# Storing the turned gated tile from the tile that held z1, and queueing the last such store behind the last stage's first loads

## The chip, the cores and the metric

The kernel runs on one core of one Trainium2 chip. Its engines work side by side, each through its own list of instructions in order: PE (TensorE, matrix products, into PSUM), ACT (ScalarE), DVE (VectorE), POOL (GpSimd) and SP (SyncE, which here only issues DMAs; POOL and ACT issue some too). They wait for each other by semaphores. The metric is the device time of one execution in microseconds (us); the number to beat is the median of three runs.

## What is computed

x is 2048 x 512, float32. It is layer-normed, and two mixers are added to it:

```python
x = A_x
xn = _layernorm(x, axis=-1)
return x + _A_ref(xn, wqkv, w_phi, wo) + _B_ref(xn, w_in, w_sp, b_sp, w_out)

# A: linear attention, 32 heads of 16
q, k, v = qkv[0], qkv[1], qkv[2]
phi_q = concat(softmax(q @ w_phi), softmax(-(q @ w_phi)))      # phi_k alike
o = phi_q (phi_k^T v) / (phi_q (phi_k^T 1) + 1e-6);   A = o @ wo

# B: gated MLP, Fh = 688
z = gelu(xn @ w_in);  z1 = z[..., :Fh];  z2 = layernorm(z[..., Fh:])
g = w_sp @ z2 + b_sp                                            # w_sp is 2048 x 2048
B = (z1 * g) @ w_out
```

## The kernel before

Rows are tiled by 128 (16 tiles, `NT`). Every float32 operand of a large product is split into two float32r parts, high and low, and a product is three matmuls (`mm3`, L53 to L55): high by high, high by low, low by high. The high part is a rounding copy (`round_h`, L45, mostly on ACT), the low part a subtraction (`rest_l`, L49, on DVE). Nearly all such work has the lines L45 and L49, so it is told apart by its tiles.

There are three stages. The first makes v, the features of k and q, and the raw z1, which goes to DRAM (`z1_d`). The middle stage makes z2 and then g = w_sp z2 by Strassen-like products of two by two blocks. The last stage, for each pair of row tiles, makes (z1 * g) @ w_out and o @ wo and adds both to x.

The part around the change is the product g and what follows it.

- g has eight steps (i = 0 to 7), each a pair of row tiles; each step has four chunks (32 chunks, `NC`). A chunk needs a pair of w_sp tiles from DRAM (`wf`, two loads of 256 KB on SP, L512, issued three chunks ahead) and their sums `S` and parts `A` (`prep_a`, on DVE and ACT, two chunks ahead). `products` gives seven PSUM tiles `g` (P1, P2, P6, P5, P7, P3, P4, made in that order), in 8 banks that are used in turn.
- At a step's end `drain` (L710 to L715) reads the seven tiles into the tile `c`: one ACT copy, then seven adds on DVE. L715 reads P7.
- `gate` (L721 to L735) multiplies that with the gelu of z1, splits off the last 48 columns, turns the whole in blocks of 32 (`dve.transpose`, L732) and stores it to DRAM (`u_d`) with four DMAs on SP, whose elements are 128 bytes. z1 comes by two loads on POOL's queue (`load_z1`, L692) into the tile tagged `z1`. Both tiles, `c` and `z1`, have one buffer. In the kernel before, the product goes into `z1`, the turned tile goes back into `c`, and the store reads `c`.
- Step 7 goes otherwise: its drained tile is kept, and its gate comes late in the last stage (`GATE_LAST`).
- During the last chunks, buffers of the operand `B` that PE has read for the last time are taken again (`slot`) for what the last stage needs first: w_out's parts, the turned tile 0 (`first_gate`: tiles `u_uh` and `ul_rt`), the normalizer `zb`, finished features of q (`first_q`: `eq`), and raw ones (`load_q`: `et`), which `q_fin` (seven DVE operations, L487 to L494, the first writing `qtmp`) finishes.
- The last stage: `project_u` (17 matmuls into `pout`), `attend_T` (16 transposes into `ptq`, L860, or L858 where the source is `et`), `attend` (products `po`, L875, copied out as `oT`), `project_o` (12 matmuls more into `pout`, with `wo`'s parts `woh` and `wol`), then the add of x and the store.

What sets the order: the program is written as loops, and a scheduler with a model of its own places the instructions of each engine; `tc.issue_after(x)` keeps what follows it behind x. DMA completions are counted in eight lanes for those that SP and ACT issue, used in turn, so that a DMA also waits for the landing of the one eight before it.

Of the kernel before, what the change touches and what calls it, by code (L numbers as in the profile page):

```python
# [10 lines left out]
F32 = mybir.dt.float32  # L11
F32R = mybir.dt.float32r
AF = mybir.ActivationFunctionType
ALU = mybir.AluOpType
# [23 lines left out]
def mixer(ctx: ExitStack, tc: tile.TileContext, x, x_t, wv, wqkT, phi_bd, wo, w_in, wst, b_r, w_out, out):  # L38
# [9 lines left out]
    def rest_l(l, src, h, eng=None):  # L48
        return (eng or dve).tensor_tensor(l, src, h.bitcast(F32), op=ALU.subtract).ins  # L49
# [427 lines left out]
    QW = NF + 7 * H  # L477

    def load_q(s, et):
        sp.dma_start(et[:, :NF + 2 * H], e_d[s])  # L480
        return et

    def q_fin(et, tmp, zb):
# [222 lines left out]
    def drain(i, g, cb):  # L706
        g = {k: t[:, :FC] for k, t in g.items()}
        b1, b2 = (bias[:, 2 * i + k:2 * i + k + 1] for k in range(2))
        c11, c12, c21, c22 = (cb[:, k] for k in range(4))
        add = lambda o, p, b, q: dve.scalar_tensor_tensor(o, p, b, q, op0=ALU.add, op1=ALU.add)  # L710
        first = act.activation(c12, g["P1"], AF.Copy)
# [3 lines left out]
        dve.tensor_tensor(c21, g["P7"], c21, op=ALU.add)  # L715
        add(c22, g["P5"], b2, c21)
        add(c12, g["P3"], b1, c12)
        drained = add(c21, g["P4"], b2, c21)
        return cb, first.ins, drained.ins

    def gate(i, cb, z, zt):  # L721
        cb, first, _ = cb
        with tc.issue_after(first):
            act.activation(z[:, :, :FH], z[:, :, :FH], AF.Gelu_apprx_tanh)
# [4 lines left out]
        dve.tensor_copy(rh, z[:, :, rm])  # L729
        rest_l(z[:, :, FH:FH + REM], z[:, :, rm], rh)  # L730
        dve.tensor_copy(z[:, :, rm], rh.bitcast(F32))
        dve.transpose(zt, z.rearrange("p k f -> p (k f)"))  # L732
        dst = u_d[2 * i:2 * i + 2].rearrange("k (j a) t -> a (k j) t", a=BL)
        for b in range(0, P, BL):
            sp.dma_start(dst[:, :, b:b + BL], zt[b:b + BL].rearrange("p (m b) -> p m b", b=BL))  # L735
# [50 lines left out]
    for n in range(NC):  # L786
        i = SEQ[n][0]
        if n % NQ == 1 and i < NP - 1:
            z = load_z1(i)
        products(n, g)  # L790
        if n % NQ == NQ - 1 and i < NP - 1:
            c = gt.tile([P, 2 * FU], F32, tag="c", name="c")
            gate(i, drain(i, g, c[:, :4 * FC].rearrange("p (a b) -> p a b", a=4)), z, c)
            g = {}
        if n + 3 < NC:
            raw[n + 3] = load_a(n + 3)
        if n + 2 < NC:
            A[n + 2] = prep_a(n + 2, raw.pop(n + 2))
        if n == NC - 4:
            stage_w()  # L800
        if n == NC - 3:
            zs = slot("zb", F32R)
            zb, ident_r = zs[:, :NF].bitcast(F32), zs[:, NF:NF + P]
            round_h(act, ident_r, ident)
            sp.dma_start(zb, zb_d)
# [14 lines left out]
    us, fin = {}, []  # L820

    def fetch_u(i):
        return load_u(i, cw.tile([P, KF, P], F32, tag="u", bufs=4, name="u"),
# [21 lines left out]
    sp.dma_start(kvT.rearrange("p g t -> p (g t)"), kvT_d)  # L845
    pst = ctx.enter_context(psum("pst", 4))
    pso = ctx.enter_context(psum("pso", 1))

    def attend_T(s):

# [69 lines left out]
    fin.append(ins)  # L920
    features(3)
    for s in (2, 3):
        us[s] = fetch_u(s)

    def ahead(i):

        if 3 < i + 3 < NT:
# [6 lines left out]
    for i in range(0, NT, 2):  # L934
# [17 lines left out]
                z = load_z1(NP - 1)  # L952
        if i == GATE_LAST:
            with tc.issue_after(lasts[0]), tc.issue_after(lasts[1]):
                gate(NP - 1, cb, z, gt.tile([P, 2 * FU], F32, tag="zt", name="zt"))
            p2.close()
        if i + 2 < NT:
            with tc.issue_after(lasts[4]):
# [34 lines left out]
```

## Time and profile before

| | |
|---|---|
| median of 3 runs | 641.39 us (641.39 to 642.18) |
| the profiled execution | 643.36 us, its span 641.6 us, granted clock 0.995 |
| PE busy | 626.9 us (98% of the span) |
| DVE busy | 517.2 us (81%) |
| ACT busy | 269.8 us (42%) |
| the product g | 283 to 499 us of the span |
| the last stage | about 499 us to the end |

PE is nearly always busy, so what can be won is where it waits or runs at a lower clock; an average over the span doesn't show those places, a list of PE's waits does. A row of the timeline is: start in us, length in us, engine, line, operation, out<-in, shapes, count; in brackets the engine's idle time before it and what ended that.

### The profile page before, as it was taken

What the parts mean: (1) busy time and instruction counts of PE and PEld (TensorE: products, weight loads), DVE (VectorE), ACT (ScalarE), POOL (GpSimd) and SP (SyncE); (2) the same over time, 40 slices, a digit from 0 to 9 for tenths busy, and PEclk for the clock granted to TensorE, in tenths of its full rate; (3) what the DMA queues carried; (4) which work ended last, traced back from release to release, by engine and by line L of the source; (5) the groups of instructions that cost most, each with busy time, mean ns of one, the idle gap of its engine ahead of it and who ended that gap; (6) DMA issues with size and microseconds to landing.
All of it is one profiled execution on the core that took longest, in us unless ns stands there. A gap on an engine that the chain in (4) does not pass through costs nothing.

```text
span 641.6 us, 11420 instructions
## 1 busy us (share of the span) xinstructions
PE 626.9 (98%) x4406; PEld 567.6 (88%) x4406; DVE 517.2 (81%) x916; ACT 269.8 (42%) x431; POOL 86.0 (13%) x168
## 2 busy tenths in 40 slices
PE   8999999999999999999999999999999699999997
PEld 6888888888889999999999999999999577777776
DVE  5999979987978779889979687696967589899822
ACT  5644434443423648876443333334334132323220
POOL 4142212111010025350000000000000001100000
PEclk9999999999999999999999999999999799999999
DMA  8445464354256930003474563827567797986930
GB/s 314 159 100 140 123 173 137 99 154 126 67 137 172 331 115 34 2 11 86 139 165 96 143 142 101 178 82 161 125 160 180 243 277 251 336 265 216 260 102 33
DMA packets 94965, 98.39 MB, mean 153 GB/s; under 512 B 52448, under 2 KB 65504, under 8 KB 94912
## 3 DMA queue, kind: packets, MB, share of 16 engines
q1 hardware_dynamic: 84992, 62.81, 35.0%
q0 software_dynamic: 7616, 29.23, 16.1%
q10 hardware_dynamic: 2304, 5.64, 2.3%
q8 instruction: 34, 0.56, 0.4%
q14 instruction: 19, 0.16, 0.1%
HBM read 56.37 MB, written 26.61 MB: 129 GB/s over the span
## 4 chain that ended last, share of the span: by engine, by line
PE 94%; DMA 2%; DVE 2%; issue 1%; SPq 0%; ACT 0%; POOL 0%; DVEq 0%; ACTq 0%; POOLq 0%
PE g L53 10%; PE g L54 10%; PE g L55 10%; PE proj L55 7%; PE proj L53 7%; PE proj L54 7%; PE zps L55 6%; PE zps L53 6%; PE zps L54 6%; PE pout L53 6%; PE pout L54 5%; PE pout L55 5%; PE po L875 2%; DMA wf<-in_wst 1%; PE ptq L860 1%; PE kvps L312 1%
## 5 line engine op out<-in xcount | busy, mean ns | idle before, releaser
L53 PE MATMUL g<-B,A 128*128 128x344 f32 x448 | 143.8, 321 | 2.3 <-DVE c L715 2.3
L54 PE MATMUL g<-B,A 128*128 128x344 f32 x448 | 143.4, 320 | 0.0
L55 PE MATMUL g<-B,A 128*128 128x344 f32 x448 | 143.0, 320 | 0.0
L53 PEld LDWEIGHTS g<-B,A 128*128 128x128 f32 x448 | 84.2, 188 | 3.7 <-DVE c L715 3.5
L54 PEld LDWEIGHTS g<-B,A 128*128 128x128 f32 x448 | 84.2, 188 | 0.0
L55 PEld LDWEIGHTS g<-B,A 128*128 128x128 f32 x448 | 84.2, 188 | 0.0
L45 ACT ACTIVATE A<-S 128x512 fp32r<-128x512 f32 x64 | 40.2, 631 | 82.0 <-DVE S L531 59.6
L113 ACT ACTIVATE e<-e,r_x 128x1024 f32<-128x1024 f32 x28 | 32.2, 1149 | 49.2 <-DVE e L112 49.2
L53 PE MATMUL proj<-wqk_h,xT 128*128 128x512 f32 x128 | 51.0, 398 | 0.0
L55 PE MATMUL proj<-wqk_h,xT 128*128 128x512 f32 x128 | 50.6, 396 | 0.0
L54 PE MATMUL proj<-wqk_l,xT 128*128 128x512 f32 x128 | 50.3, 393 | 0.0
L49 DVE TENSOR_TENSOR A<-S,A 128x512 fp32r<-128x512 f32 x64 | 43.8, 686 | 5.7 <-ACT A L45 5.5
L53 PE MATMUL zps<-w_0h,xT 128*128 128x344 f32 x128 | 41.5, 324 | 0.0
L55 PE MATMUL zps<-w_0h,xT 128*128 128x344 f32 x128 | 41.2, 322 | 0.0
L53 PE MATMUL zps<-w_1h,xT 128*128 128x344 f32 x128 | 41.1, 321 | 0.0
L55 PE MATMUL zps<-w_1h,xT 128*128 128x344 f32 x128 | 40.9, 320 | 0.0
L54 PE MATMUL zps<-w_0l,xT 128*128 128x344 f32 x128 | 40.9, 320 | 0.0
L54 PE MATMUL zps<-w_1l,xT 128*128 128x344 f32 x128 | 40.9, 319 | 0.0
L45 ACT ACTIVATE A<-wf 128x512 fp32r<-128x512 f32 x64 | 31.7, 515 | 20.1 <-PE g L55 10.0
L116 DVE TENSOR_REDUCE sm<-e 128x64 f32<-128x1024 f32 x28 | 33.9, 1209 | 4.9 <-ACT e L113 4.8
L530 DVE TENSOR_TENSOR S<-wf 128x256 f32<-128x256 f32 x32 | 13.4, 420 | 29.6 <-DMA wf<-in_wst 29.6
L49 DVE TENSOR_TENSOR A<-wf,A 128x512 fp32r<-128x512 f32 x64 | 35.3, 552 | 2.3 <-ACT A L45 2.0
(202 smaller groups left out, 1414.2 us busy)
## 6 DMA issues: line engine op xcount, KB each, us to landing
wf<-in_wst SPq DMA_DIRECT2D x64, 256.0 KB, 3.8
e_d<-e POOLq DMA_DIRECT2D x16, 544.0 KB, 5.1
et<-e_d SPq DMA_DIRECT2D x16, 544.0 KB, 5.8
zacc<-e POOLq DMA_DIRECT2D x12, 512.0 KB, 4.7
er<-et POOLq DMA_DIRECT2D x12, 512.0 KB, 4.7
z_d<-z1f ACTq DMA_DIRECT2D x16, 344.0 KB, 3.2
z1t<-z_d POOLq DMA_DIRECT2D x16, 344.0 KB, 5.2
u_d<-c SPq DMA_DIRECT2D x28, 184.0 KB, 6.9
```

What stands on the lines that cost most here:

```text
L45: return act.activation(h, src, AF.Copy).ins
L49: return (eng or dve).tensor_tensor(l, src, h.bitcast(F32), op=ALU.subtract).ins
L53: pe.matmul(dst, ah, bh, start=start, stop=False)
L54: pe.matmul(dst, ah, bl, start=False, stop=False)
L55: return pe.matmul(dst, al, bh, start=False, stop=stop).ins
L113: act.activation(e, e, AF.Exp, scale=scale)
L116: dve.tensor_reduce(sm, heads(e), axis=AX.X, op=ALU.add)
L312: i = pe.matmul(kv_acc[k:k + QP, m // 4], vs[:, m * QP:(m + 1) * QP], e[:, m * HP:(m + 1) * HP], start=first and m < 4 and len(ready) == n ...
L530: dve.tensor_tensor(sums[:, 0], b[:, 0], b[:, 1], op=ALU.add)
L860: pe.transpose(pt[:, a, k].bitcast(F32R), src, ident_r)
L875: lasts[3] = pe.matmul(po[r][c * QP:(c + 1) * QP, k], kvT[rows, m // 2, cols], fs[m // 4][rows, m // 2 % 2], start=True, stop=True).ins
```

## The change

1. `gate` takes two tiles more by name: the product goes into the tile of the drained sums (`u`, that is `c`), and the turned tile into `ut`, which is z1's own tile `z`. The store therefore reads `z1`'s buffer instead of `c`'s. For step 7 the product stays in `z`, as before.
2. `gate` returns its store as a function. Steps 0 to 5 call it at once. Step 6's store is called after the first loads of the last stage: tiles 0 and 1 of `u_d`, two finished and two raw tiles of q.
3. These loads are put together differently: tile 1 of `u_d` goes to a slot of its own (`u1`) ahead of the last chunk, instead of a buffer of the last stage; `q_fin` of tile 2 stands behind the drain of step 7.
4. `wo` comes by four loads of 128 rows instead of sixteen of 32 rows; the loads of tiles 2 and 3 of `u_d` stand ahead of it.
5. The PSUM pool of `pout` and `po` is opened ahead of that of `ptq`, so that it takes the first banks that the product g leaves.

The core of the diff:

```diff
 def load_q(s, et):
-    sp.dma_start(et[:, :NF + 2 * H], e_d[s])
+    load_q.last = sp.dma_start(et[:, :NF + 2 * H], e_d[s]).ins
...
-    def gate(i, cb, z, zt):
+    def gate(i, cb, z, u, ut):
...
-        dve.tensor_tensor(zs, zs, cb.rearrange("p (k j) f -> p k j f", k=2), op=ALU.mult)
+        us = u[:, :, :FH].rearrange("p k (j f) -> p k j f", j=2)
+        dve.tensor_tensor(us, zs, cb, op=ALU.mult)
...
-        dve.transpose(zt, z.rearrange("p k f -> p (k f)"))
-        dst = u_d[2 * i:2 * i + 2].rearrange("k (j a) t -> a (k j) t", a=BL)
-        for b in range(0, P, BL):
-            sp.dma_start(dst[:, :, b:b + BL], zt[b:b + BL].rearrange("p (m b) -> p m b", b=BL))
+        dve.transpose(ut.rearrange("p k f -> p (k f)"), u.rearrange("p k f -> p (k f)"))
+        def store():
+            src = ut.rearrange("p k f -> p (k f)")
+            dst = u_d[2 * i:2 * i + 2].rearrange("k (j a) t -> a (k j) t", a=BL)
+            for b in range(0, P, BL):
+                sp.dma_start(dst[:, :, b:b + BL], src[b:b + BL].rearrange("p (m b) -> p m b", b=BL))
+        return store
...
-            c = gt.tile([P, 2 * FU], F32, tag="c", name="c")
-            gate(i, drain(i, g, c[:, :4 * FC].rearrange("p (a b) -> p a b", a=4)), z, c)
+            c = gt.tile([P, 2, FU], F32, tag="c", name="c")
+            cq = c[:, :, :FH].rearrange("p k (j f) -> p k j f", j=2)
+            store = gate(i, drain(i, g, cq), z, c, z)
+            if i < NP - 2:
+                store()
...
             uT = [first_gate(0)]
-            ets[2] = load_q(2, slot("et"))
-            es[2], last = q_fin(ets.pop(2), slot("qtmp")[:, :NF], zb)
+            es[0], es[1] = first_q(0), first_q(1)
         if n == NC - 2:
-            es[0], es[1] = first_q(0), first_q(1)
-            ets[3] = load_q(3, slot("et"))
-    cb = drain(NP - 1, g, slot("c").rearrange("p (a b) -> p a b", a=4))
+            t = slot("u1", F32R)
+            us = {1: load_u(1, k_tiles(t[:, :KF * P]).bitcast(F32), t[:2 * REM, KF * P:(KF + 1) * P])}
+            ets[2], ets[3] = (load_q(s, slot("et")) for s in (2, 3))
+            with tc.issue_after(load_q.last):
+                store()
+    cb = drain(NP - 1, g, slot("c").rearrange("p (k j f) -> p k j f", k=2, j=2))
+    with tc.issue_after(cb[1]), tc.issue_after(cb[2]):
+        es[2], last = q_fin(ets.pop(2), slot("qtmp")[:, :NF], zb)
...
-    us[1] = fetch_u(1)
...
-    pst = ctx.enter_context(psum("pst", 4))
     pso = ctx.enter_context(psum("pso", 1))
+    pst = ctx.enter_context(psum("pst", 4))
...
+    for s in (2, 3):
+        us[s] = fetch_u(s)
...
         for c in range(ND):
-            rows = [(m * QP, (m + 1) * QP) for m in range(c // 2 * 8 + c % 2, (c // 2 + 1) * 8, 2)]
-            load_w(wo, rows, wo_h[:, c], wo_l[:, c], cw.tile([P, D], F32, tag="wof", bufs=4, name="wof"))
+            t = cw.tile([P, D], F32, tag="wof", bufs=4, name="wof")
+            sp.dma_start(t, wo.rearrange("(k m a r) d -> k a m r d", k=2, a=2, r=QP)[c // 2, c % 2])
+            round_h(act, wo_h[:, c], t)
+            rest_l(wo_l[:, c], t, wo_h[:, c])
```

What this does to the order, first on SP's queue from the last chunks of g into the last stage. In the kernel before (`zb` is the normalizer, `u_d<-c` the store of step 6; behind the last row come the sixteen loads of wo):

```order
L805 DMA zb<-zb_d 128x1024
L735 DMA u_d<-c 32x46x32 x4
L750 DMA u_uh<-u_d 128x5x128
L751 DMA ul_rt<-u_d 96x128
L480 DMA et<-e_d 128x1088
L772 DMA eq<-e_d 128x1024 x2
L480 DMA et<-e_d 128x1088
L750 DMA u<-u_d 128x5x128
L751 DMA rt<-u_d 96x128
L845 DMA kvT<-kvT_d 128x512
```

And in the changed kernel, from the same load of `zb` on (`u_5477` is the slot `u1`; behind the last row come four loads of `u` and `rt` for tiles 2 and 3, and then the four loads of wo):

```order
L812 DMA zb<-zb_d 128x1024
L754 DMA u_uh<-u_d 128x5x128
L755 DMA ul_rt<-u_d 96x128
L776 DMA eq<-e_d 128x1024 x2
L754 DMA u_5477<-u_d 128x5x128
L755 DMA u_5477<-u_d 96x128
L480 DMA et<-e_d 128x1088 x2
L739 DMA u_d<-z1t 32x46x32 x4
L855 DMA kvT<-kvT_d 128x512
```

The four DMAs of the store moved from ahead of seven loads to behind them, and wo has four issues where there were sixteen.

Second, DVE at the drain of step 7 (`c<-g`). Before, the operations of `q_fin` of tile 2 (`qtmp`, `et`) stand ahead of it and between its adds:

```order
L49 TENSOR_TENSOR ul_rt<-u_uh 128x640
L487 TENSOR_TENSOR qtmp<-et,zb 128x1024
L488 TENSOR_REDUCE et<-qtmp 128x64
L710 SCALAR_TENSOR_TENSOR c<-g,bias,c 128x344
L713 TENSOR_TENSOR c<-g,c 128x344
L489 TENSOR_TENSOR et<-et 128x64
L714 TENSOR_TENSOR c<-g,c 128x344
L490 SCALAR_TENSOR_TENSOR et<-et 128x32
L715 TENSOR_TENSOR c<-g,c 128x344
```

In the changed kernel, from the same `ul_rt` on, the last split of an operand `A`, the whole drain, and only then `q_fin`:

```order
L49 TENSOR_TENSOR ul_rt<-u_uh 128x640
L49 TENSOR_TENSOR A<-S,A 128x512
L710 SCALAR_TENSOR_TENSOR c<-g,bias,c 128x344
L713 TENSOR_TENSOR c<-g,c 128x344
L714 TENSOR_TENSOR c<-g,c 128x344
L715 TENSOR_TENSOR c<-g,c 128x344
L710 SCALAR_TENSOR_TENSOR c<-g,bias,c 128x344 x3
L487 TENSOR_TENSOR qtmp<-et,zb 128x1024
L49 TENSOR_TENSOR ul<-u_5477,uh 128x640
L488 TENSOR_REDUCE et<-qtmp 128x64
```

The drain went ahead of `q_fin`; on ACT likewise the rounding of `u_uh` went one place forward, ahead of the last rounding of an `A`.

Third, DVE at the first pair of the last stage, from the first `oT` on. Before, the two adds of x (`xr<-pout`) stand inside `q_fin` of tile 3:

```order
L49 TENSOR_TENSOR oT<-po,oT 128x2x256 x2
L487 TENSOR_TENSOR qtmp<-et,zb 128x1024
L488 TENSOR_REDUCE et<-qtmp 128x64
L489 TENSOR_TENSOR et<-et 128x64
L906 TENSOR_TENSOR xr<-pout,xr 128x512
L490 SCALAR_TENSOR_TENSOR et<-et 128x32
L491 RECIPROCAL et<-et 128x32
L492 TENSOR_TENSOR et<-et 128x64
L906 TENSOR_TENSOR xr<-pout,xr 128x512
L494 TENSOR_TENSOR et<-et 128x1024
```

In the changed kernel they stand behind it and behind the first operation of tile 4's:

```order
L49 TENSOR_TENSOR oT<-po,oT 128x2x256 x2
L487 TENSOR_TENSOR qtmp<-et,zb 128x1024
L488 TENSOR_REDUCE et<-qtmp 128x64
L489 TENSOR_TENSOR et<-et 128x64
L490 SCALAR_TENSOR_TENSOR et<-et 128x32
L491 RECIPROCAL et<-et 128x32
L492 TENSOR_TENSOR et<-et 128x64
L494 TENSOR_TENSOR et<-et 128x1024
L487 TENSOR_TENSOR qtmp<-et,zb 128x1024
L916 TENSOR_TENSOR xr<-pout,xr 128x512 x2
```

So the adds that empty the first two `pout` moved five operations back. PE's list at this place has the sixteen transposes of the next pair in one piece ahead of `project_u`, where before four stood ahead of it and twelve behind it. In steps 0 to 5 of g the order on every engine is as before; what differs there are the tiles.

More of the change, by code (lines that the diff above doesn't have):

```diff
@@ L708, in drain @@
         b1, b2 = (bias[:, 2 * i + k:2 * i + k + 1] for k in range(2))
-        c11, c12, c21, c22 = (cb[:, k] for k in range(4))
+        c11, c12, c21, c22 = (cb[:, k, j] for k in range(2) for j in range(2))
         add = lambda o, p, b, q: dve.scalar_tensor_tensor(o, p, b, q, op0=ALU.add, op1=ALU.add)
@@ L725, in gate @@
         zs = z[:, :, :FH].rearrange("p k (j f) -> p k j f", j=2)
[L726 removed]
+        us = u[:, :, :FH].rearrange("p k (j f) -> p k j f", j=2)
+        dve.tensor_tensor(us, zs, cb, op=ALU.mult)
         rm = slice(KF * P, FH)
         rh = gt.tile([P, 2, REM], F32R, tag="rh", name="rh")
[L729 to L735 removed]
+        dve.tensor_copy(rh, u[:, :, rm])
+        rest_l(u[:, :, FH:FH + REM], u[:, :, rm], rh)
+        dve.tensor_copy(u[:, :, rm], rh.bitcast(F32))
+        dve.transpose(ut.rearrange("p k f -> p (k f)"), u.rearrange("p k f -> p (k f)"))
[5 more added lines that the diff above has]
+        return store
     def slot(name, dt=F32):
@@ L819, in mixer @@
     wk = ctx.enter_context(left("cwk", 2))
-    us, fin = {}, []
+    fin = []
     def fetch_u(i):
@@ L845, in mixer @@
     sp.dma_start(kvT.rearrange("p g t -> p (g t)"), kvT_d)
+    pso = ctx.enter_context(psum("pso", 1))
     pst = ctx.enter_context(psum("pst", 4))
-    pso = ctx.enter_context(psum("pso", 1))
     def attend_T(s):
@@ L921, in mixer @@
     features(3)
-    for s in (2, 3):
-        us[s] = fetch_u(s)
     def ahead(i):
@@ L954, in mixer @@
             with tc.issue_after(lasts[0]), tc.issue_after(lasts[1]):
-                gate(NP - 1, cb, z, gt.tile([P, 2 * FU], F32, tag="zt", name="zt"))
+                gate(NP - 1, cb, z, z, gt.tile([P, 2, FU], F32, tag="zt", name="zt"))()
             p2.close()
```

## The prediction

> **What bounds the kernel now.** I read the page first, then the waits of PE, then the timelines of PE, DVE, SP and ACT where g gives way to the last stage, and last one boundary between two steps of g. The page: the span, and the granted clock in 40 slices.
>
> ```profile
> span 641.6 us, 11420 instructions
> PEclk9999999999999999999999999999999799999999
> ```
>
> One slice of 16 us (497 to 513) has a lower clock. PE's waits, longest first, name the same place at their head, and another one behind it:
>
> ```profile
> PE pout L53 <- DVE c L715: 5.8, 1, 5.8
> PE g L53 <- DVE c L715: 2.3, 4, 0.7
> ```
>
> The first is the start of the last stage, the second are four boundaries between steps of g. The timeline of PE at the first (start, length):
>
> ```profile
> 498.62 0.32 PE L55 MATMUL g<-B,A 128*128 128x344 f32 x1
> 504.78 0.77 PE L53 MATMUL pout<-wu,u_uh 128*128 128x512 f32 x1 [5.84 <-DVE c L715]
> ...
> 511.32 1.48 PE L860 MATMUL ptq<-zb,eq 128*128 128x128 f32 x16
> 512.63 0.46 PE L53 MATMUL pout<-wu,uh 128*128 128x512 f32 x1
> ...
> 516.74 1.09 PE L875 MATMUL po<-f,kvT 64*32 64x256 f32 x32
> 518.57 0.50 PE L53 MATMUL pout<-woh,oT 128*128 128x512 f32 x1 [0.74 <-ACT oT L45]
> ```
>
> PE stands for 5.84 us. Then the first `project_u` takes 511.32 - 504.78 = 6.54 us, and the second, the same 17 matmuls, 516.74 - 512.63 = 4.11 us. Stretches with the granted clock (after the counts) tell why:
>
> ```profile
> 476.00:498.00 22.00, 22.00 (x140) 22.00 (x141) 17.27 (x33) 8.20 (x16) 0.00 (x0) 1.00 0.76 188
> 504.00:508.00 4.00, 3.22 (x8) 2.58 (x9) 4.00 (x10) 0.74 (x1) 0.00 (x0) 0.50 0.57 155
> 512.00:516.00 4.00, 4.00 (x25) 3.39 (x24) 1.58 (x3) 4.00 (x9) 0.00 (x0) 1.00 0.85 247
> ```
>
> Full clock to the end of g, half after the stand, full again later: 6.54 - 4.11 = 2.43 us more lost. Why PE stands, from DVE:
>
> ```profile
> 497.15 0.83 DVE L49 TENSOR_TENSOR ul_rt<-u_uh 128x640 fp32r<-128x640 f32 x1 [4.61 <-ACT u_uh L45]
> 500.01 1.23 DVE L487 TENSOR_TENSOR qtmp<-et,zb 128x1024 f32<-128x1024 f32 x1 [2.03 <-DMA eq<-e_d]
> ...
> 502.40 0.57 DVE L710 SCALAR_TENSOR_TENSOR c<-g,bias,c 128x344 f32<-128x344 f32 x1
> ...
> 504.12 0.52 DVE L715 TENSOR_TENSOR c<-g,c 128x344 f32<-128x344 f32 x1
> ```
>
> DVE sits in its order before `qtmp`, whose tile `et` lands at 500.0; the drain stands behind that, and PE's first `pout` waits for the bank that L715 empties. The late landing comes from SP's queue:
>
> ```profile
> 483.81 0.34 SPq L805 DMA_DIRECT2D zb<-zb_d  x1
> 487.47 4.57 SPq L735 DMA_DIRECT2D u_d<-c  x4
> 492.13 0.65 SPq L750 DMA_DIRECT2D u_uh<-u_d  x1
> ...
> 498.96 11.56 SPq L745 DMA_DIRECT2D wof<-in_wo  x16
> ```
>
> From 484.15 to 487.47 the queue waits for step 6's turned tile, then issues its store for 4.57 us; all first loads come behind. Note the sixteen issues of wo: 11.56 us.
>
> **The change, part by part.** *Drain ahead of `q_fin`, last store behind the first loads.* `u_uh`, `ul_rt` and the two `eq` follow `zb` as soon as PE frees their slots, within the chunk that ends near 485.6 (a chunk is 42 matmuls of 22 / 140 = 0.157 us, 6.6 us, and the last ends at 498.9). So `u_uh` is issued about 7.5 us earlier. The drain's add of P7 then waits for nothing but P7, which PE ends about 2 us before the last product; the adds behind it are done some 0.7 us after the last product. PE needs none of these for its first `pout`: it starts when g ends. Gain 5.84 us, and with no stand the clock stays, as it does over the 0.74 at 518.57 and the 0.7 of the boundaries: 2.43 us. Together 8.27 us. ACT now rounds `u_uh` ahead of the last `A`; the A has room, since its product comes 3.8 us into the last chunk (496.1) and `u_uh` should land by 490.
>
> *What is late next.* `project_u(0)` would run from 498.9 to 503.0, the transposes to 504.3, `project_u(1)` to 508.4, `po` to 509.5, `project_o` from 510.3 (518.57 - 8.27). It needs wo's parts:
>
> ```profile
> 513.73 2.21 ACT L45 ACTIVATE woh<-wof 128x512 fp32r<-128x512 f32 x4
> ```
>
> Tile 1's `u`, before the last of the loads behind the store, is now issued near 487 and lands long before DVE wants it. The store then goes out at about 491.2, when PE has freed the slots of both `et`, and lands 7.0 us later (below); kvT, tiles 2 and 3 and the four loads of wo follow, wo issued about 499.8 to 501.4 and landed by about 506, as four 256 KB loads behind a store take 4.4 to 4.7 us (the wf row below). ACT reaches `woh` behind four copies at about 505.5 and is done at 507.7: some 2.5 us to spare. The four loads instead of sixteen save no time by themselves here (before, woh waited for ACT, not for wo), but the earlier `woh` needs them: sixteen issues of 0.72 us would end past 510. Taken: 0; bounds 0 and 1.5 us lost, if the queue runs 4 us later.
>
> *PSUM banks.* With the drain done 0.7 us after g, the order of the pools decides at most that 0.7 us. Inside the 8.27.
>
> *The turned tile in z1's buffer*, six boundaries. Before (one boundary; SP, POOL, ACT, DVE, PE):
>
> ```profile
> 458.98 6.49 SPq L735 DMA_DIRECT2D u_d<-c  x4
> 459.48 1.07 POOL L692 DMA_DIRECT2D z1t<-z_d  x2 [26.29 <-DVE S L531]
> 468.49 0.46 ACT L711 ACTIVATE c<-g 128x344 f32<-128x344 f32 x1 [2.84 <-DMA u_d<-c]
> 468.84 1.34 ACT L724 ACTIVATE z1t<-z1t 128x1376 f32<-128x1376 f32 x1
> 470.08 0.62 ACT L45 ACTIVATE A<-wf 128x512 fp32r<-128x512 f32 x1
> 471.51 0.42 DVE L530 TENSOR_TENSOR S<-wf 128x256 f32<-128x256 f32 x1 [5.40 <-DMA wf<-in_wst]
> 473.77 0.68 DVE L49 TENSOR_TENSOR A<-wf,A 128x512 fp32r<-128x512 f32 x1
> 475.39 0.51 DVE L715 TENSOR_TENSOR c<-g,c 128x344 f32<-128x344 f32 x1
> 475.96 0.42 PE L53 MATMUL g<-B,A 128*128 128x344 f32 x1 [0.42 <-DVE c L715]
> ```
>
> The chain that ends in PE's wait is store, wf loads behind it, DVE's sums, drain. The change frees `c` early, which ends ACT's 2.84 us of waiting, worth nothing since DVE is later. But it makes POOL's load of z1 wait for the store, and all that ACT holds behind the gelu waits too. Landings, of the last store (no z1 load beside it), of the one above, and of that z1 load and the four wf behind it:
>
> ```profile
> L735 SPq DMA_DIRECT2D u_d<-c x4: 322/884/2329, 487.5 to 489.7; - x4
> DMA to landing us min/median/max: 2.8/4.2/4.7
> ...
> L735 SPq DMA_DIRECT2D u_d<-c x4: 325/932/4168, 459.0 to 461.3; - x4
> DMA to landing us min/median/max: 2.9/6.9/7.3
> ...
> DMA to landing us min/median/max: 4.8/5.0/5.2
> ...
> DMA to landing us min/median/max: 4.4/4.5/4.7
> ```
>
> Alone, a store is down 489.7 + 4.7 - 487.5 = 7.0 us after its first issue; with z1 beside it 9.4 (468.4, since ACT's copy at 468.49 waited for it, less 459.0). So now: store down at 459.0 + 7.0 = 466.0; z1's second load issued 0.6 later (half of 1.07, and 0.1), landed 5.0 later, 471.6; gelu, `A<-wf` 1.24 later (470.08 - 468.84) and 0.62 long, DVE's L49 at 473.5 against 473.77. The wf loads come some 2 us earlier, so L530 no longer decides. Net about 0.2 earlier per boundary, 0.1 us for each of the four that PE feels: 0.5 in all. Bounds: 2.3 us gained (all four waits), 3 us lost (z1 half a us later at six boundaries).
>
> *The last stage's first pairs.* The matmuls `po` at the first two pairs of whole length, and at a later one:
>
> ```profile
> 529.93 1.88 PE L875 MATMUL po<-f,kvT 64*32 64x256 f32 x32
> 546.60 2.10 PE L875 MATMUL po<-f,kvT 64*32 64x256 f32 x32
> 579.49 1.09 PE L875 MATMUL po<-f,kvT 64*32 64x256 f32 x32
> ```
>
> Twice 0.8 to 1.0 us are lost because twelve transposes stand right ahead of `po`, which waits for their copies. With all sixteen ahead of `project_u` that should go: 1.8 us. Against it, DVE's two adds of x now come behind `q_fin` of tile 3 and its next operation; PE needs their `pout` back for the third `project_u`. By DVE's lengths (1.2 us for each of the three long operations, about 1.1 for the four short ones) they end near 518.2, `project_o` near 516, transposes take 1.3: a wait of 0.5 to 1 us, and the copy `er` for tile 5 may come as late again. Taken: 0.5 gained; bounds 1.8 gained, 1 lost.
>
> Sum: 8.27 + 0.5 + 0.5 = 9.3 us. The profiled execution took 643.36 (span 641.6), 1.97 above the median; the sum is a difference within its span, and I take it off the median: 641.39 - 9.3 = 632.1. A change under 0.2% (1.3 us) can't be told from none.
>
> **Rivals.**
> *A, slower: z1 lands late at every boundary.* Behind the store it meets four wf loads of 256 KB, and ACT, then DVE, then PE wait. z1 beside the store cost the store 9.4 - 7.0 = 2.4 us, so that much engine time it needs; if the wf loads halve its rate throughout, it lands 2.4 us later, PE goes on at 478.1 instead of 475.96, six times 2.2 = 13 us lost: 641.39 - 8.8 + 13 = 645.6. It decides from 1.5 us per boundary (8.8 / 6). Against it: z1 beside the store landed in 4.8 to 5.2, and most of the wf bytes have gone by when z1's start. The Trainium skill, DMA: Bandwidth & Descriptors, Queues, rings and completion order, says that a DMA engine goes round robin between the queues it has work for, a packet at a time; by that z1 would share evenly with wf, which have large packets, and did better beside the store because those are small. This is this rival, 645.6 by it if the overlap were full. No row here shows z1 beside four wf.
>
> *B: PE waits for loads instead.* The DMA queue is the true bound, wo or tile 2 lands some 4 us later than I say, and `project_o` starts at 513 to 514 instead of 510.3: 641.39 - 9.3 + 3.5 = 635.6. For it: the 0.85 DMA share of the windows row. Against: 3.3 us of idle queue ahead of the old store are now used. The Trainium skill, TensorE: Matmul & The Clock Gate, What's actually happening, puts the drop to half clock at an idle window of about 3.4 us; by it such a wait could bring the half clock back, which no row between 0.74 and 5.84 shows, and would add up to the 2.43 above.
>
> *C, better:* the boundaries' 2.3 and the whole 1.8 of the last stage are won: 641.39 - 8.27 - 4.1 = 629.0.
>
> *D: no change.* DVE's drain was not what held PE, and operands come as late: the 497.15 row says they were there 6.8 us before PE started.
>
> **Numbers.** My forecast 0.58 (632.1, own range 630 to 634.5), C 0.15, B 0.15, A 0.09 (its mild half still near the old time), D 0.03. The range, 628.8 to 638.5, holds C and B and A's mildest. Faster 0.88, same 0.03, slower 0.09.
>
> **What would show it.** Right: no wait of PE at the first `pout`, full clock in the windows after it, `project_o` 8 us nearer to the end of g; DVE's drain directly behind g; PE's waits at boundaries under 2.3 us in all, ACT's waits there now for DMA z1. Wrong: PE's `g` waiting over 1 us at each of six boundaries (A), or `pout<-woh` waiting for `woh`, `uh` or a DMA (B), or `pout` for `xr` by over 1 us.

## The result, and the profile after

The changed kernel took 652.5 us (median of four runs, 652.0 to 654.18), the kernel before, on the same chip, 641.78 (641.39 to 642.37). The ratio is 1.0171, with a 95% interval of 1.0149 to 1.0192: 10.7 us slower, where 9.3 faster was forecast. The page of the kernel after, the span and the granted clock in 40 slices:

```profile
span 650.4 us, 11408 instructions
PEclk9999999999999999999999998999899969999999
```

The low slice is still there, one further on, and two slices within g are now a little low. The waits of PE in the kernel after (us in total, times, longest):

```profile
PE pout L53 <- ACT oT L45: 9.9, 1, 9.9
PE g L53 <- DVE c L715: 6.6, 4, 2.7
```

The wait of the first `pout` for the drain, 5.84 us before, is gone. A wait of 9.9 us for `oT` stands in its place, a little later, and the waits of g at the boundaries went from 2.3 to 6.6 us. The timeline of PE where g ends:

```profile
506.14 0.32 PE L55 MATMUL g<-B,A 128*128 128x344 f32 x1
506.30 0.40 PE L53 MATMUL pout<-wu,u_uh 128*128 128x512 f32 x1
...
515.65 1.09 PE L885 MATMUL po<-f,kvT 64*32 64x256 f32 x32
526.62 0.79 PE L53 MATMUL pout<-woh,oT 128*128 128x512 f32 x1 [9.87 <-ACT oT L45]
```

PE goes from g to the last stage without a pause, and `po` starts 9.2 us after g's end at 506.46; before it was 17.8 us (498.94 to 516.74). So what the change was to win there, it won. But `project_o`, the `pout` with `woh`, starts 20.2 us after g's end, no earlier than before (19.6). From there to the end it is 123.8 us, before 123.0.

What `oT` stood behind, from ACT's timeline:

```profile
511.10 0.74 ACT L45 ACTIVATE uh<-u 128x640 fp32r<-128x640 f32 x1 [8.55 <-DMA u<-u_d]
511.74 2.04 ACT L872 ACTIVATE f<-ptq 128x512 f32<-128x512 f32 x4
515.65 0.63 ACT L45 ACTIVATE woh<-wof 128x512 fp32r<-128x512 f32 x1 [1.87 <-DMA wof<-in_wo]
518.89 0.63 ACT L45 ACTIVATE woh<-wof 128x512 fp32r<-128x512 f32 x1 [2.61 <-DMA wof<-in_wo]
521.63 0.63 ACT L45 ACTIVATE woh<-wof 128x512 fp32r<-128x512 f32 x1 [2.11 <-DMA wof<-in_wo]
524.83 0.63 ACT L45 ACTIVATE woh<-wof 128x512 fp32r<-128x512 f32 x1 [2.57 <-DMA wof<-in_wo]
```

Each of the four copies waits for its load, and the loads come in some 3 us apart. Stretches of the same kernel (busy time of PE, PEld, DVE, ACT, POOL; then granted clock, DMA share, GB/s):

```profile
504.00:508.00 4.00, 4.00 (x24) 3.69 (x23) 3.24 (x6) 0.00 (x0) 0.00 (x0) 1.00 1.10 147
512.00:516.00 4.00, 4.00 (x33) 2.98 (x39) 2.83 (x6) 2.13 (x5) 0.00 (x0) 1.00 0.26 92
524.00:528.00 4.00, 1.38 (x3) 1.16 (x4) 2.51 (x4) 2.23 (x4) 0.00 (x0) 0.50 0.69 212
```

In the second of these stretches, while hardly anything but wo's loads is under way, the DMA share is 0.26, at 92 GB/s. That is the work of four of the 16 engines, and the trace's packets say the same: of 200 moments between 512 and 516 us, 162 have four packets under way at once, 36 five, two six, and none fewer than four. The last row shows that the stand brings the half clock back.

The other loss is within g, which ends at 506.46 instead of 498.94. One boundary in the kernel after (SP, POOL, ACT, DVE, PE):

```profile
436.02 5.13 SPq L739 DMA_DIRECT2D u_d<-z1t  x4
444.25 1.06 POOL L692 DMA_DIRECT2D z1t<-z_d  x2 [28.51 <-DMA u_d<-z1t]
451.16 1.36 ACT L724 ACTIVATE z1t<-z1t 128x1376 f32<-128x1376 f32 x1 [7.53 <-DMA z1t<-z_d]
452.42 0.61 ACT L45 ACTIVATE A<-wf 128x512 fp32r<-128x512 f32 x1
453.06 0.69 DVE L49 TENSOR_TENSOR A<-wf,A 128x512 fp32r<-128x512 f32 x1 [3.12 <-ACT A L45]
454.69 0.51 DVE L715 TENSOR_TENSOR c<-g,c 128x344 f32<-128x344 f32 x1
455.26 0.43 PE L53 MATMUL g<-B,A 128*128 128x344 f32 x1 [2.68 <-DVE c L715]
```

It is a chain: z1's load starts only when the store has landed, 8.2 us after the store's first issue; ACT's gelu waits 7.53 us for it; the copy `A` stands behind the gelu in ACT's order, the subtraction of `A` waits for the copy on DVE, the drain's L715 stands behind that, and PE waits for the bank. Over the six boundaries ACT now waits for z1 34.6 us, a wait that the kernel before doesn't have:

```profile
ACT z1t L724 <- DMA z1t<-z_d: 34.6, 6, 7.5
```

The clock behind this stand, and behind one of 1.81 us at 396.87:

```profile
397.00:400.00 3.00, 3.00 (x14) 3.00 (x15) 3.00 (x8) 0.00 (x0) 0.00 (x0) 0.66 0.17 51
455.00:458.00 3.00, 2.74 (x12) 2.74 (x13) 3.00 (x8) 0.00 (x0) 0.00 (x0) 0.67 0.29 80
```

Each of the two times the clock is at half for 3.41 us. PE has work throughout, but its matmuls start every 0.287 us instead of 0.157, which loses 1.5 us each time.

### The profile page after: what moved, and what is told of

The parts are those of the page before. It is cut to its first block, busy times and chain, and to the rows that moved or that the text cites. A ratio compares the mean times of both kernels' runs of the same rounds, so it can differ in the third digit from the quotient of the medians.

```text
span 650.4 us, 11408 instructions
## 1 busy us (share of the span) xinstructions
PE 627.9 (97%) x4406; PEld 569.9 (88%) x4406; DVE 518.4 (80%) x916; ACT 269.0 (41%) x431; POOL 86.2 (13%) x168
## 4 chain that ended last, share of the span: by engine, by line
PE 86%; DMA 7%; DVE 3%; issue 2%; SPq 1%; ACT 1%; POOL 0%; ACTq 0%; POOLq 0%; DVEq 0%
PE g L53 9%; PE g L55 9%; PE g L54 9%; PE proj L55 7%; PE proj L53 7%; PE proj L54 7%; PE zps L55 6%; PE zps L53 6%; PE zps L54 6%; PE pout L53 4%; PE pout L54 4%; PE pout L55 4%; DMA wof<-in_wo 2%; DMA z1t<-z_d 2%; DMA et<-e_d 1%
## 5 line engine op out<-in xcount | busy, mean ns | idle before, releaser
L53 PEld LDWEIGHTS g<-B,A 128*128 128x128 f32 x448 | 85.3, 190 | 8.0 <-DVE c L715 8.0
L54 PEld LDWEIGHTS g<-B,A 128*128 128x128 f32 x448 | 85.3, 190 | 0.0
L55 PEld LDWEIGHTS g<-B,A 128*128 128x128 f32 x448 | 85.3, 190 | 0.0
L53 PE MATMUL pout<-woh,oT 128*128 128x512 f32 x60 | 24.6, 410 | 9.9 <-ACT oT L45 9.9
```

Of the source, the lines that this page charges most:

```text
L53: pe.matmul(dst, ah, bh, start=start, stop=False)
L54: pe.matmul(dst, ah, bl, start=False, stop=False)
L55: return pe.matmul(dst, al, bh, start=False, stop=stop).ins
```

## The experiments

Two questions come first: what the shape of wo's loads costs, and what the store from z1's tile costs. Then: do both losses, taken away, leave the forecast's gain, and which part of the change made it? In the expectations T1 (or theory 1) is the explanation that a run is to test. The two kernels with flat loads of wo leave out the right pairing of wo's rows with the product: they do the same amounts of work and measure a time, but compute another result.

| kernel | us | ratio to before | 95% interval |
|---|---|---|---|
| after | 652.5 | 1.0171 | 1.0149 to 1.0192 |
| after, wo in sixteen loads (`e1_wo16`) | 647.98 | 1.0079 | 1.0058 to 1.0099 |
| after, wo in four flat loads (`e2_woflat`) | 643.42 | 1.0024 | 1.0014 to 1.0034 |
| after, store from c (`e3_cstore`) | 644.93 | 1.0041 | 1.0027 to 1.0055 |
| `e1` and `e3` together (`e4_both`) | 638.57 | 0.9939 | 0.9916 to 0.9961 |
| `e2` and `e3` together (`e5_flat_both`) | 634.78 | 0.9893 | 0.9866 to 0.9921 |
| `e4`, PSUM order undone (`e7_pst`) | 637.62 | 0.9930 | 0.9908 to 0.9952 |
| `e4`, `q_fin` ahead again (`e8_qfin`) | 640.53 | 0.9967 | 0.9949 to 0.9984 |
| `e4`, both of these undone (`e10_both_undone`) | 639.62 | 0.9966 | 0.9951 to 0.9980 |
| `e4`, tiles 2 and 3 behind wo (`e12_fetchback`) | 638.42 | 0.9948 | 0.9931 to 0.9965 |
| `e4`, wo on POOL's queue (`e13_poolwo`) | 636.22 | 0.9907 | 0.9892 to 0.9923 |
| `e13` and `e12` together (`e16_pool_fb`) | 636.27 | 0.9907 | 0.9886 to 0.9927 |
| `e1`, store on two queues (`e15_split`) | 643.18 | 1.0018 | 0.9998 to 1.0039 |

### wo in sixteen loads again

```diff
-            sp.dma_start(t, wo.rearrange("(k m a r) d -> k a m r d", k=2, a=2, r=QP)[c // 2, c % 2])
+            for m in range(4):
+                sp.dma_start(t[m * QP:(m + 1) * QP], wo.rearrange(...)[c // 2, c % 2, m])
```

> The changed kernel, with wo in sixteen loads of 32 rows again; all else as changed. Theory 1 (the four loads of wo, whose source has an outermost dimension of 4, are moved by few of the DMA engines: in the profile after, the DMA share is 0.26 and 92 GB/s while they are waited for): PE's stand of 9.9 us ahead of the first product with woh goes to under 3 us, and the clock behind it stays up; 652.5 - 8 to 11 = 641.5 to 644.5 us. Rival (rival B of the prediction: the queue is late as a whole, by the store and the loads ahead of wo): the stand stays at 8 us or more, since sixteen issues come no sooner than four; 651 to 654 us. The stands at the boundaries of g stay at 6 to 7 us in all under both.

It took 647.98, between the two. The waits of PE:

```profile
PE g L53 <- DVE c L715: 7.0, 5, 2.2
PE pout L53 <- ACT oT L45: 4.4, 1, 4.4
```

The stand at `woh` fell from 9.9 to 4.4 us, not to the under 3 that was expected: the sixteen loads are issued between 510.6 and 519.5 us and land between 515 and 521, one after the other. The waits within g stayed.

### wo in four loads of neighbouring rows

```diff
-            sp.dma_start(t, wo.rearrange("(k m a r) d -> k a m r d", k=2, a=2, r=QP)[c // 2, c % 2])
+            sp.dma_start(t, wo[c * P:(c + 1) * P, :])
```

> The changed kernel, with the four loads of wo at the same places and of the same 256 KB, but each from 128 rows that follow each other (so the rows of wo are in another order than the product needs: what is left out is the right pairing of wo's rows; all amounts of work are the same). Theory 1 (the shape of the source): the four land within about 3 us of each other, the stand ahead of woh goes to under 2 us; 641 to 643.5 us, a little under the kernel with sixteen loads. Rival (the queue is late as a whole): the stand stays near 9.9 us, 651 to 654 us.

643.42, within the expected range. ACT's copies of wo, and a stretch at the same place:

```profile
514.62 2.71 ACT L45 ACTIVATE woh<-wof 128x512 fp32r<-128x512 f32 x4 [0.69 <-DMA wof<-in_wo]
```

```profile
512.00:516.00 4.00, 4.00 (x46) 2.70 (x44) 3.67 (x8) 3.23 (x7) 0.00 (x0) 1.00 1.02 362
```

The same four loads of 256 KB, with another order of rows, land 5.2 to 5.9 us after their issue, with the DMA engines full; the copies wait 0.7 us once. The stand is 2.4 us, a little over the 2 that was expected, and the time 9.1 us less. So neither the count nor the size of the loads was the fault, but the shape of their source: in the changed kernel its outermost dimension is four groups of 32 rows, here it is 128 rows, and the DMA share goes from 0.26 to 1.02. The Trainium skill, DMA: Bandwidth & Descriptors, Rules for kernel authors, says that an outermost dimension of fewer than 16 confines the whole transfer to at most that many DMA engines; the trace agrees, with 0.26 of 16 engines busy for an outermost dimension of four.

### The store from c again

```diff
-            store = gate(i, drain(i, g, cq), z, c, z)
+            store = gate(i, drain(i, g, cq), z, z, c)
```

> The changed kernel, but steps 0 to 6 of g put the product into z1's tile and store the turned tile from c's, as before; wo in four loads as changed. Theory 2 (z1's load waits for the store, then ACT, DVE and PE for it, at the boundaries of g): g ends near 499 us of the span instead of 506.5, PE's waits at the boundaries fall from 6.6 to about 2.3 us; 652.5 - 7.5 = 645 us, within 1. Rival (the boundaries are later for another reason, such as the changed layout of c): g still ends near 506, 651 to 654 us. The 9.9 us ahead of woh stay under both.

644.93, as expected: 7.6 us of the loss. The waits of PE:

```profile
PE pout L53 <- ACT oT L45: 10.9, 1, 10.9
PE g L53 <- DVE c L715: 1.7, 3, 0.7
```

g ends at 498.3 again, within 0.7 us of before, and 8.1 earlier than in the kernel after. Of these 8.1 us, 4.9 are shorter stands (6.6 against 1.7), and some 3.1 the two stretches at half clock that are gone.

### Both together

```diff
-            store = gate(i, drain(i, g, cq), z, c, z)
+            store = gate(i, drain(i, g, cq), z, z, c)
...
-            sp.dma_start(t, wo.rearrange(...)[c // 2, c % 2])
+            for m in range(4):
+                sp.dma_start(t[m * QP:(m + 1) * QP], wo.rearrange(...)[c // 2, c % 2, m])
```

> Both together: store from c's tile, and wo in sixteen loads; what is left of the change is the order of the first loads, the drain ahead of q_fin and the order of the PSUM pools. Theories 1 and 2: their gains add, 652.5 - 7.5 - 9 to 11 = 634 to 636 us; by the prediction's sum without its boundaries 641.8 - 8.3 - 0.5 = 633 us. If the queue is the bound (rival B), 640 us or more.

638.57: faster than the kernel before, but 2.6 us above the upper end of what was expected. What is left is a stand of 3.8 us at `project_o`. ACT's rows there:

```profile
503.97 0.74 ACT L45 ACTIVATE uh<-u 128x640 fp32r<-128x640 f32 x1 [8.70 <-DMA u<-u_d]
...
507.47 0.63 ACT L45 ACTIVATE woh<-wof 128x512 fp32r<-128x512 f32 x1 [0.81 <-DMA wof<-in_wo]
508.44 0.63 ACT L45 ACTIVATE woh<-wof 128x512 fp32r<-128x512 f32 x1 [0.34 <-DMA wof<-in_wo]
...
512.08 0.63 ACT L45 ACTIVATE woh<-wof 128x512 fp32r<-128x512 f32 x1 [1.06 <-DMA wof<-in_wo]
512.62 1.07 ACT L45 ACTIVATE oT<-po 128x512 fp32r<-128x512 f32 x2
```

Two suspects: tile 2's `u`, which lands 4.8 us after g's end (499.19), and wo's sixteen loads, for which the copies wait 2.9 us in all.

### Which of the two is late: three kernels

The first takes the flat loads of wo together with the store from c:

```diff
-            for m in range(4):
-                sp.dma_start(t[m * QP:(m + 1) * QP], wo.rearrange(...)[c // 2, c % 2, m])
+            sp.dma_start(t, wo[c * P:(c + 1) * P, :])
```

> The kernel with the product in z1's tile and the store from c (638.57 in its own runs), with wo now in four loads of 128 neighbouring rows each (it therefore pairs other rows of wo with the product than the reference does; work and bytes are the same). T1, that what is left ahead of project_o is the landing of sixteen loads one by one: the stand of TensorE at the first pout with woh falls from 3.8 to about 2 us, as it fell from 4.4 to 2.4 with the store from z1's tile, and the time is 636.0 to 637.2. Rival, that tile 2's u, landed 4.9 us after the end of g, holds the copies behind it whatever wo does: the stand stays at 3.5 to 4 and the time is 638.2 to 639.

634.78, a little better than T1. PE's rows:

```profile
497.50 0.32 PE L55 MATMUL g<-B,A 128*128 128x344 f32 x1
...
508.86 0.50 PE L53 MATMUL pout<-woh,oT 128*128 128x512 f32 x1 [0.76 <-ACT oT L45]
```

A stand of 0.76, at full clock, and `project_o` 11.0 us after g's end, against 19.6 before. Tile 2's `u` is nearly as late here as in the kernel above (ACT's copy of it starts 4.4 us after g's end, there 4.8), and that costs no more than these 0.76 us.

The second leaves the sixteen loads and issues them on POOL's queue:

```diff
-                sp.dma_start(t[m * QP:(m + 1) * QP], wo.rearrange(...)[c // 2, c % 2, m])
+                pool.dma_start(t[m * QP:(m + 1) * QP], wo.rearrange(...)[c // 2, c % 2, m])
```

> The same kernel (638.57) with wo's sixteen loads issued on POOL's queue in place of SP's, so that they don't stand behind the store and tile 2's u there. T1, that project_o waits for wo because its loads are issued last on SP's queue: wo has landed 3 us or more earlier, the stand at the first pout with woh falls below 2 us, and the time is 635 to 637. Rival, that tile 2's u holds the copies (it lands 4.9 us after the end of g): stand 3 to 4 us and 638 to 639. If POOL issues a load every 0.5 us only from the end of g on, wo lands no earlier than on SP and the stand stays as well; u and wo are then told apart by which of them the copies of wo wait for.

636.22, within T1's range, and 5.95 us under the kernel before on that chip (642.17). The waits of PE:

```profile
PE pout L53 <- ACT oT L45: 1.5, 1, 1.5
PE pout L54 <- DVE wol L49: 1.3, 1, 1.3
PE pout L53 <- DVE xr L916: 1.0, 1, 1.0
```

POOL begins to issue 1.6 us before g's end, and the first loads land at 500.1. One stand of 3.8 has become three of 1.0 to 1.5, behind none of which the clock falls. Of the kernels that take every row of wo where the reference has it, none is faster.

The third puts tiles 2 and 3 behind wo on SP, as before:

```diff
-    for s in (2, 3):
-        us[s] = fetch_u(s)
     wo_h, wo_l = (cw.tile([P, ND, D], F32R, name=f"wo{k}") for k in "hl")
...
     features(3)
+    for s in (2, 3):
+        us[s] = fetch_u(s)
```

> The kernel with sixteen wo loads and the store from c (638.57), with the loads of tiles 2 and 3 behind wo again, as before. T1, that wo is late because those four loads and their issue stand ahead of it on SP, and that tile 2's u, which lands 4.9 us after the end of g, holds the copies of wo on ScalarE: woh no longer waits behind uh, the stand at the first pout with woh falls from 3.8 to 0.5 to 1.5, and the time is 635 to 637. Rival, that tile 2's u is now the late one: TensorE waits for it at its project_u by 1 to 4 us, and the time is 637.5 to 641.

638.42, no gain, and the stand at `woh` is 4.9 us. wo comes earlier, but ACT's rows show what is late now:

```profile
507.51 0.63 ACT L45 ACTIVATE woh<-wof 128x512 fp32r<-128x512 f32 x1 [1.22 <-DMA wof<-in_wo]
509.58 0.74 ACT L45 ACTIVATE uh<-u 128x640 fp32r<-128x640 f32 x1 [1.44 <-DMA u<-u_d]
511.66 0.74 ACT L45 ACTIVATE uh<-u 128x640 fp32r<-128x640 f32 x1 [1.34 <-DMA u<-u_d]
512.30 1.07 ACT L45 ACTIVATE oT<-po 128x512 fp32r<-128x512 f32 x2
```

The copy `oT`, which PE needs, stands in ACT's order behind two `uh` that PE doesn't need yet. The time is in the rival's range, but PE doesn't wait for tile 2's `u` itself: it waits for what ACT holds behind it. The same written order with wo on POOL, its diff the two above together:

> The kernel with the store from c and wo's sixteen loads on POOL's queue (636.22), with the loads of tiles 2 and 3 written behind wo as before, which now stand on another queue than wo. T1, that tile 2's u held the copies there (it landed at 505.15 with ScalarE waiting 11.0 us): only the place in the order of issue changes, the same loads stand in the same places of SP's queue, so the time is 635.5 to 637, the same. Rival, that the written order moves u behind other work on SP: TensorE waits for tile 2 and the time is 637.5 or more.

636.27, the same as with POOL alone, as T1 said.

### Which part made the gain: three kernels

In the kernel with sixteen loads and the store from c, the order of the PSUM pools is undone, then the place of `q_fin`, then both:

```diff
-    pso = ctx.enter_context(psum("pso", 1))
     pst = ctx.enter_context(psum("pst", 4))
+    pso = ctx.enter_context(psum("pso", 1))
```

```diff
             es[0], es[1] = first_q(0), first_q(1)
+            es[2], last = q_fin(ets.pop(2), slot("qtmp")[:, :NF], zb)
...
-    with tc.issue_after(cb[1]), tc.issue_after(cb[2]):
-        es[2], last = q_fin(ets.pop(2), slot("qtmp")[:, :NF], zb)
```

> The same kernel (638.57) with the order of the two PSUM pools undone: pst's four banks taken ahead of pso's one. T1, that the drain directly behind g frees the banks at once whatever their order: the first pout waits 0.8 us at most, the time is 638.4 to 639.5. Rival, that the bank that the first pout gets is what took its wait away: it waits some 2 us or more, the clock falls to half behind it, and the time is 641 to 646.

> The same kernel (638.57) with tile 2's q_fin written ahead of the drain again; VectorE then has its subtractions, sums and products (4.65 us in all) between the four steps of the drain. T1, that the output banks taken first make the drain's lateness harmless for the first pout: no wait there, tile 2's ul a little later, the time 638.4 to 639.6. Rival, that the drain's place behind g on VectorE carries the forecast's gain: the first pout, or the first ptq, waits 2 to 5 us and the clock falls behind it, the time is 642 to 647.

> The kernel with sixteen wo loads and the store from c (638.57), with two parts undone together: tile 2's q_fin ahead of the drain (640.53 alone, no wait at the first pout) and pst's banks ahead of pso's (637.62 alone, no wait there either). T1, that each of the two alone keeps the first pout from waiting, since the drain with q_fin between its steps ends 2.9 us after the end of g and matters only to banks that the drain frees: with both undone the first pout waits 1.5 to 3 us, the clock falls for some 3 us behind it, and the time is 642 to 645.5. Rival, that the wait of 5.84 us before came from elsewhere (from what VectorE waited for, the late et): no wait, and 640 to 641.5.

637.62, 640.53 and 639.62: all three lie outside their T1's ranges, by 0.8 to 2.4 us, and no interval is clear of the others' by much. So the times alone say only that nothing here is worth several us. The rows say more. With the pools' order undone the first `pout` waits for nothing. With `q_fin` ahead, g ends at 498.35 and the drain at 501.07, 2.7 us later, and yet the first `pout` starts without a wait, at 498.19. With both undone it waits:

```profile
499.71 0.50 PE L53 MATMUL pout<-wu,u_uh 128*128 128x512 f32 x1 [1.34 <-DVE c L715]
```

Either of the two parts is enough for the first `pout`, and without both the wait is 1.34 us, less than the 1.5 to 3 of T1 and too short to lower the clock. Before it was 5.84 with the same places of `q_fin` and of the pools. What stays changed there is the order of the first loads on SP, ahead of the last store: before, `q_fin` waited for its `et` until 500.0, after g's end, and here it starts at 495.2, 3.2 us ahead of it. So some 4.5 of the 5.84 us, and the half clock, go to the order of the loads; this is read from these rows, as no kernel changes that order alone. Why the second kernel's time is 2 us above the one it was made from is not settled; the stand at its `project_o` is the same 3.8 us.

### The boundary: waiting for the store, or for the loads beside z1's

```diff
-                sp.dma_start(dst[:, :, b:b + BL], src[b:b + BL]...)
+                (pool if b >= P // 2 else sp).dma_start(dst[:, :, b:b + BL], src[b:b + BL]...)
```

> The kernel with sixteen wo loads and the store from z1's tile (647.98, g's end at 507.4, TensorE's g waiting 7.0 us), with two of each store's four DMAs issued on POOL's queue in place of SP's. T1, that z1 waits for the landing of the store's last DMA (issued 3.3 us after the first on SP): z1's loads are issued 1.5 to 2 us earlier, the waits of g fall below 3 us with most of their half clock, g ends at 500 to 503 and the time is 641 to 644.5. Rival, that the lateness is contention of z1's load with the wf loads beside it (it took 6.0 us and not the 5.0 of before): the issue may come earlier but the landing doesn't, and the time stays at 647 to 649. Two more of POOL's issues could also cost as much as they save; the issue times tell that.

643.18, and g ends at 503.4 instead of 507.4: T1's range, though not by T1's reason. The waits of g, which T1 had below 3 us, are nearly those of before (7.0):

```profile
PE g L53 <- DVE c L715: 6.5, 5, 2.2
```

z1's loads are issued no earlier (9.2 and 9.8 us after the store's first issue at the boundary that the expectation took, against 8.1 and 8.6), but they are shorter. The landing of z1's fourteen loads within g, of the kernel with the store on one queue, then on two:

```profile
L692 POOL DMA_DIRECT2D z1t<-z_d x14: 538/538/628, 302.8 to 474.5; - x14
...
DMA to landing us min/median/max: 4.2/5.7/7.8
```

```profile
L692 POOL DMA_DIRECT2D z1t<-z_d x14: 547/561/628, 302.7 to 472.0; - x14
...
DMA to landing us min/median/max: 3.1/4.3/5.1
```

With two of the store's DMAs on POOL, SP is free for the `wf` loads sooner; more of them have landed when z1's loads start, and those take 4.3 us instead of 5.7. Contention with `wf` is thus part of z1's lateness, as the rival said, and the wait for the store the rest of it. But what the loads gain they lose again by their later issue: z1 is down 13.3 to 14.5 us after the store's first issue, against 13.9 to 16.2, and PE's stands are only 0.5 us shorter. The rest of the 4.0 us is the clock. In the kernel with one queue it is at half for 3.41 us twice within g, behind the stands that end at 370.25 and 456.20; here it stays up throughout g. That is some 3.1 us, and with the 0.5 it makes 3.6 of the 4.0. So this run doesn't show that a second queue shortens the wait for the store. By the chain above a second buffer for z1 would take that wait away; this was not tried.

## Why the prediction was wrong

**The stand at the first `pout`: right.** It is gone, the clock stays at 1.00, and `po` comes 8.6 us nearer to g's end, against 8.27 in the sum. The working gave this to the drain's place behind g; the runs give some 4.5 of the 5.84 to the order of the loads on SP, with the drain's place and the banks as two ways to remove the last 1.3. That the order of the banks decides "at most that 0.7 us" held.

**What is late next: wrong, and the larger error.** The step reads: wo "issued about 499.8 to 501.4 and landed by about 506, as four 256 KB loads behind a store take 4.4 to 4.7 us", "Taken: 0; bounds 0 and 1.5 us lost". The price came from a row of loads of the same size and another shape. Measured, each load took some 3 us of its own on four engines, one behind the other; the shape costs 9.1 us (after, against four flat loads) or 10.2 (the same pair with the store from c). At 92 GB/s the 1 MB of wo takes some 11 us; that the source is four groups of 32 rows could be read in the kernel, and I didn't weigh it. A smaller part of the same step failed too: the issue came 3.1 us after g's end, not 0.9, since the last store took 6.97 us to issue, not 4.57; why it did is open. With flat loads a stand of 2.4 us is left, or of 0.8 with the store from c.

**The boundaries: the mechanism was seen, its size wrong, and the sign with it.** The sum was 7.0 for the store, 0.6 for the issue, 5.0 for the load: 12.6 us from the store's first issue to z1. At the boundary shown it was 8.75 to the second issue and 6.3 for the load, 15.07 in all, and 13.9 to 15.1 at the six. Half of the error is the load, priced from rows without `wf` beside it. The store from z1's tile costs 7.6 to 9.4 us (after against `e3`, `e1` against `e4`), of which some 3.1 are the clock, at half behind two of the four stands; the working has no such term at the boundaries. It is rival A's mechanism, which had 0.09. It said z1 2.4 us later per boundary, and 1.3 to 2.5 came; its 13 us for the six were too many, but the 1.3 to 1.6 per boundary that were lost lie at the 1.5 from which it decides. Its evidence against, that most of the `wf` bytes are gone when z1's loads start, was wrong: at that boundary three `wf` loads land at 446.4 to 448.7, and z1's are issued at 444.3 and 444.8.

**Rival B** named the place of the larger loss, `woh` waiting for its DMA, and the half clock behind it; its price of 3.5 us was a third of what came, and its cause, the DMA queue as the bound, was not the one: the DMA share was 0.26 while wo came in.

**The last stage's first pairs:** no gain to be seen, within the bounds given: 123.8 us from `project_o` to the end, 123.0 before. The 123.8 begin with 4.5 us at half clock, but in the kernel without the two losses, at full clock, it is 123.4. The wait for `xr` came, with 0.4 us in the kernel after and 1.6 in the one without the two losses.

**The sum.** With the two losses taken away, the pairing of wo's rows left out and all else kept, the kernel took 634.78, which is 1.07% under the kernel before (0.79 to 1.34%), where 1.45% was forecast. So the terms of gain that this kernel keeps, 8.27 and 0.5, came to 7.4 us instead of 8.8. The two other terms, wo taken as nothing and the boundaries as a gain of 0.5, cost 652.5 - 634.78 = 17.7 together.

## What to carry to other kernels

A load's price is that of its shape, not of its size: before a row is used as a price, see that its outermost dimension is the same, and look at the DMA share while it runs. A transfer that now starts behind another's landing is to be priced with what else is on the queues at its new time, and the chain behind it followed through every engine's order, to the engine that can't wait. A stand is to be priced with the clock behind it, also a short one. Where a step must be late anyway, a second issuing queue or another order of the first loads can be the smaller edit: here the kernel with wo on POOL's queue and the store from c, at 0.9907 of the time before, is better than both kernels that were compared.

## What the hardware showed that was not expected

The clock falls behind shorter stands than the 5.84 us that the profile of before shows. Of the stands of PE of over 0.25 us between 330 and 540 us in these fourteen kernels, none up to 1.64 us was followed by half pace (matmuls of g starting every 0.29 us instead of 0.157). Of the eight between 1.81 and 2.48, five were. All ten of 2.68 to 10.92 were, for 3 to 5.5 us from their end. Two of nearly the same place, in the kernel after

```profile
396.87 0.43 PE L53 MATMUL g<-B,A 128*128 128x344 f32 x1 [1.81 <-DVE c L715]
```

with the clock at 0.66 behind it (above), and in the one with the store on two queues, a longer stand with the clock kept:

```profile
397.02 0.43 PE L53 MATMUL g<-B,A 128*128 128x344 f32 x1 [2.18 <-DVE c L715]
```

The length of a stand doesn't settle it, then, and the traces' records of the granted clock say what does, nearly. In each of the fourteen, every change of the clock lies a whole number of times 3.413 us behind the first one, and the low stretches ahead of the kernel's end are 3.41, 6.83, 10.24 or 13.65 us long. So time is cut into slots of 3.413 us, which lie where they lie: the first change comes between 5.1 and 7.6 us of the span. What counts is how much of a stand falls into one slot. Two neighbouring slots each, first of the kernel after, at the stand of 1.81 us, then of the one with two queues, at that of 2.18:

```profile
394.56:397.97 3.41, 1.60 (x11) 1.31 (x10) 3.30 (x7) 1.94 (x5) 0.00 (x0) 1.00 0.28 77
397.98:401.39 3.41, 3.41 (x14) 3.41 (x13) 3.41 (x7) 0.00 (x0) 0.00 (x0) 0.50 0.23 61
```

```profile
393.27:396.68 3.41, 1.57 (x11) 1.29 (x9) 1.86 (x4) 3.38 (x6) 0.00 (x0) 1.00 0.03 10
396.68:400.09 3.41, 3.07 (x19) 3.07 (x20) 3.41 (x9) 0.00 (x0) 0.00 (x0) 1.00 0.25 70
```

The slot's end cuts the second stand into 1.84 and 0.34 us, and the other two of the eight without half pace into 1.41 and 0.78 (of 2.19) and 1.64 and 0.84 (of 2.48). Of all slots at full clock between 330 and 540 us, those in which PE stands for up to 1.64 us in all are followed by full clock, and all 14 with 2.04 us or more by half. In between lie the 1.81 with a fall and the 1.84 without, so the limit is near half a slot, and something beside PE's standing time weighs there; what that is stays open. A stand of about 2 us can therefore cost 1.5 us more in one trace than in another, by where it falls.

The Trainium skill, TensorE: Matmul & The Clock Gate, What's actually happening, gives a free-running window of about 3.4 us, of which an idle one lowers the clock. The traces agree on the window, 3.413 us, and that it runs free; a window that must be idle throughout does not fit a fall behind 1.81 us.
